# Attending the first batch in halves of queries, with early operands transposed by DMA and weights cast by GpSimd's DMA

## The chip, the cores and the metric

One core of one Trainium2 chip runs the kernel. The metric is the device time in microseconds (us) of one launch. All runs quoted are in the fast state, except where the text says otherwise. "Step" below is one exponential of 128 x 768 scores on ACT (ScalarE); a head pair of one batch takes 12 of them. PE is TensorE, DVE is VectorE, POOL is GpSimd, SP is SyncE (which only issues DMAs here).

## The reference, cut to what matters

Hash-bucketed attention feeds two matrix products ("the experts") with an activation between them.

```python
# q, k, v [4 batches, 8 heads, 768, 64], proj [64, 6]
q_bucket = sum_k 2**k * ((q @ proj)[..., k] > 0)        # likewise k_bucket
scores = where(q_bucket[:, None] == k_bucket[None, :], q @ k.T / 8, -1e9)
attn   = softmax(scores) @ v                            # -> x [3072, 512]
h      = x @ w_in                                       # w_in [512, 2048]
g      = h + sin(alpha * h)**2 / (alpha + 1e-9)
out    = g @ w_out                                      # w_out [2048, 512]
```

## The kernel before

There are 16 pairs (batch, two heads). For each, the kernel needs `qa` and `ka`: q and k transposed (64 rows), with 12 rows of hash bits and their complements appended, so that one matmul of 76 rows gives score and mask together. Pairs 0 to 5 are prepared on PE (hash, pick the bits, 24 transposes, four copies out of PSUM); later pairs are transposed by DMA while PE does other work. A batch's experts run after the first pair of the next batch has been attended, so before the first experts there are five pairs, 60 steps. The second product (`contract`) is dripped between the steps of the following batch by `fill`.

```python
def load_w(n):                       # 16 pieces, float32, issued by SP
    if n < 8:
        t = w_pool.tile([128, NP, 256], FP32, name="w32")
        ...
    nc.sync.dma_start(out=t, in_=src)
    return dst, t
def cast_w(dst, t, engine):          # engine is GpSimd
    engine.tensor_copy(out=dst, in_=t)

def prepare_on_pe(i):                # pairs 0 to 5
    ...                              # DVE turns q, k; GpSimd casts them into nat
    hash_into(ps, turned)            # 16 matmuls
    ...                              # DVE: bits; PE: 24 small matmuls pick rows; DVE: into nat
    for h in range(2):
        for t in (0, 1):
            out = ps[0:KA, t, 0:HALF].bitcast(BF16)
            for s in range(SB):
                nc.tensor.transpose(out[:, s * 128:(s + 1) * 128], nat[:, s, 2 * t + h], ident)
            nc.vector.tensor_copy(out=aug[t][0:KA, h, :], in_=out)
            yield
    ...

def attend(i, at_step, lag=3):
    for n in range(2 * SB):          # 12 steps
        hh, kb = divmod(n, SB)
        sc, _ = slot()               # two PSUM banks out of 0 to 5
        for half in range(2):
            nc.tensor.matmul(out=sc[:, half, 0:HALF],
                lhsT=ka[0:KA, hh, kb * 128:(kb + 1) * 128],
                rhs=qa[0:KA, hh, half * HALF:(half + 1) * HALF], start=True, stop=True)
        nc.scalar.activation(out=e..., in_=sc[:, :, 0:HALF], func=AF.Exp, scale=SCALE)
        at_step(n)                   # loads, preparation, second product
        ...                          # the exponential of three steps ago weighs v

def expand(b, at_chunk):             # first product and activation, 16 turns
    for F in range(NF):
        h = banks[:, 6:8, :] if F in (3, 7, 11) else slot()[0]
        ...                          # 8 matmuls, Sin, square, g

for i in range(n_pairs):
    attend(i, at_step)
    if hp == 0 and b > 0:
        drain()
        expand(b - 1, at_chunk)      # its last turn queues contract(b - 1)
```

The softmax here doesn't subtract the row's maximum and nothing guards it: scores larger than these inputs give would overflow.

## Time and profile before

| | us |
|---|---|
| median of 4 runs | 315.44 (312.86 to 318.0) |
| profiled span | 311.2 |
| first exponential | 10.7 |
| first matmul of the experts (after 60 steps) | 60.3 |
| next exponential | 85.5 |
| exponential number 108 (the first after batch 1's experts) | 156.7 |

The page of the kernel before, its parts 1, 2 and 4: busy time of each engine; then forty equal slices of the span with the busy share in tenths, the granted clock of PE and the share of the DMA engines; then the chain of waits by engine.

```profile
span 311.2 us, 7698 instructions
...
PE 300.7 (97%) x3055; PEld 184.3 (59%) x3055; DVE 203.5 (65%) x348; ACT 237.8 (76%) x295; POOL 97.4 (31%) x180
...
PE   7899999999989999999999999999999999999996
...
PEclk9999999999999999999999999999999999999999
DMA  7935989999628588881027587860013311200021
...
PE 73%; DVE 9%; DMA 5%; ACT 5%; POOL 3%; issue 2%; SPq 1%; DVEq 0%; ACTq 0%; POOLq 0%
```

PE is busy throughout (97%), 73% of the chain is PE.

The view by windows of the kernel before, cut at the stages of the table. Columns: window and its length, then busy us (and instructions) of each engine, granted clock, DMA share, GB/s.

```profile
core 0: us, PE busy (x) PEld busy (x) DVE busy (x) ACT busy (x) POOL busy (x), PEclk, DMA share, GB/s
0.00:10.70 10.70, 8.37 (x113) 7.25 (x114) 5.58 (x17) 2.29 (x4) 7.50 (x25) 1.00 0.85 278
10.70:60.30 49.60, 47.05 (x805) 34.20 (x804) 35.86 (x72) 43.95 (x59) 35.03 (x65) 1.00 0.83 222
60.30:85.50 25.20, 25.01 (x169) 14.66 (x166) 22.64 (x30) 22.94 (x27) 11.13 (x11) 1.00 0.89 265
85.50:156.70 71.20, 70.37 (x677) 41.51 (x676) 50.22 (x85) 59.45 (x73) 29.27 (x54) 1.00 0.57 133
156.70:311.20 154.50, 149.92 (x1303) 86.71 (x1300) 89.22 (x148) 109.16 (x135) 14.49 (x27) 1.00 0.34 83
```

### The profile page before, as it was taken

How to read it: one execution, taken by the hardware profiler on the slowest of the kernel's cores; microseconds unless marked ns; L12 is line 12 of the kernel's file. 1: busy time of each engine (PE TensorE's matmuls, PEld its weight loads, DVE VectorE, ACT ScalarE, POOL GpSimd, SP SyncE). 2: the span in 40 equal slices, each digit the busy share in tenths (PEclk: the TensorE clock that was granted, in tenths of full speed). 3: DMA queues.
4: the chain of work that ended last, by engine and by line, in shares of the span. 5: the costliest groups of instructions: out<-in, count | busy, mean ns of one | idle time of the engine just before them, and what ended most of it. 6: DMA issues, size and time to landing. Idle time of an engine off the chain costs nothing.

```text
span 311.2 us, 7698 instructions
## 1 busy us (share of the span) xinstructions
PE 300.7 (97%) x3055; PEld 184.3 (59%) x3055; DVE 203.5 (65%) x348; ACT 237.8 (76%) x295; POOL 97.4 (31%) x180
## 2 busy tenths in 40 slices
PE   7899999999989999999999999999999999999996
PEld 6567767666555565666555565566555655565444
DVE  5587576799956656679955744669974424499411
ACT  1679989899887787789897787789897877599200
POOL 6748398426594433515000524410000000000000
PEclk9999999999999999999999999999999999999999
DMA  7935989999628588881027587860013311200021
GB/s 238 377 126 138 241 276 282 185 290 293 209 71 223 94 220 207 148 225 26 2 69 194 122 223 127 205 115 7 2 56 51 105 28 69 59 2 0 35 102 68
DMA packets 68724, 42.87 MB, mean 138 GB/s; under 512 B 46560, under 2 KB 63696, under 8 KB 68688
## 3 DMA queue, kind: packets, MB, share of 16 engines
q1 hardware_dynamic: 68576, 42.37, 52.5%
q8 instruction: 24, 0.39, 0.6%
q14 instruction: 12, 0.10, 0.1%
q10 hardware_dynamic: 112, 0.01, 0.0%
HBM read 28.01 MB, written 7.27 MB: 113 GB/s over the span
## 4 chain that ended last, share of the span: by engine, by line
PE 73%; DVE 9%; DMA 5%; ACT 5%; POOL 3%; issue 2%; SPq 1%; DVEq 0%; ACTq 0%; POOLq 0%
PE banks L432 24%; PE banks L467 22%; PE banks L397 13%; PE banks L377 8%; ACT e L404 5%; PE banks L193 3%; DMA v_3085<-in_v_dram 2%; DVE g L419 2%; PE banks L269 2%; DVE osb L475 1%; DMA k_148<-in_k_dram 1%; DMA ka<-kn 1%; DMA xt<-xn 1%; DVE qt L184 1%; DVE xn L351 1%
## 5 line engine op out<-in xcount | busy, mean ns | idle before, releaser
L404 ACT ACTIVATE e<-banks 128x768 bf16<-128x768 f32 x192 | 147.6, 811 | 32.0 <-PE banks L397 24.2
L467 PE MATMUL banks<-w_out_bf,g 128*128 128x512 bf16 (+1 forms) x400 | 103.8, 370 | 1.4 <-DVE osb L475 1.0
L397 PE MATMUL banks<-qa,ka 76*128 76x384 bf16 x384 | 92.6, 325 | 1.4 <-DVE g L419 0.7
L432 PE MATMUL banks<-xt,w_in_bf 128*128 128x384 bf16 x512 | 85.3, 326 | 0.4 <-DMA xt<-xn 0.2
L377 PEld LDWEIGHTS <-e 128*128 128x128 bf16 x1152 | 55.2, 97 | 27.4 <-issue 0.3
L432 PEld LDWEIGHTS <-w_in_bf 128*128 128x128 bf16 x512 | 49.7, 98 | 33.8 <-issue 1.2
L441 ACT ACTIVATE s<-banks,alpha_sb 128x768 bf16<-128x768 f32 x64 | 57.1, 893 | 11.5 <-PE banks L432 10.6
L377 PE MATMUL banks<-vaug,e 128*128 128x65 bf16 x1152 | 61.5, 193 | 0.0
L467 PEld LDWEIGHTS <-g 128*128 128x128 bf16 x400 | 38.5, 97 | 33.5 <-issue 3.1
L345 DVE TENSOR_TENSOR total<-banks,base 128x390 f32<-128x390 f32 x28 | 15.7, 561 | 39.8 <-PE banks L377 39.6
L475 DVE COPY osb<-banks 128x512 f32<-128x512 f32 (+1 forms) x25 | 16.7, 668 | 28.4 <-PE banks L467 28.4
L397 PEld LDWEIGHTS <-ka 76*128 76x128 bf16 x384 | 28.5, 98 | 10.7 <-issue 2.0
L210 POOL TENSOR_TENSOR vacc<-vacc,vaug 128x130 f32<-128x130 f32 x48 | 21.5, 448 | 3.8
L351 DVE TENSOR_TENSOR xn<-total,rden 128x384 bf16<-128x384 f32 x28 | 17.3, 618 | 1.0
L193 PE MATMUL banks<-qt,w_hash 128*32 128x192 f32 x128 | 13.6, 332 | 1.3 <-ACT e L404 0.5
L193 PE MATMUL banks<-kt,w_hash 128*32 128x192 f32 x128 | 13.5, 332 | 0.0
L269 PEld LDWEIGHTS <-nat 128*76 128x76 bf16 x144 | 10.4, 114 | 3.7 <-POOL nat L228 0.8
L269 PE MATMUL banks<-ident,nat 128*76 128x128 bf16 x144 | 11.5, 219 | 1.1 <-DVE nat L256 0.7
L273 DVE COPY qa<-banks 76x768 bf16<-76x768 bf16 x12 | 6.5, 546 | 5.7 <-PE banks L269 5.7
L193 PEld LDWEIGHTS banks<-qt,w_hash 128*32 128x32 f32 x128 | 5.9, 109 | 7.4 <-issue 2.5
L309 DVE TENSOR_SCALAR bits<-banks,side 128x192 bf16<-128x192 f32 x20 | 7.4, 412 | 3.2 <-ACT e L404 3.2
L203 POOL CAST vaug<-v_2876 128x768 bf16<-128x768 f32 x1 | 0.8, 829 | 25.4 <-PE banks L377 25.4
(275 smaller groups left out, 289.4 us busy)
## 6 DMA issues: line engine op xcount, KB each, us to landing
out_dram<-osb SPq DMA_DIRECT2D x23, 256.0 KB
rows<-bits SPq DMA_DIRECT2D x40, 24.0 KB
w_697<-in_moe_w_in_dram SPq DMA_DIRECT2D x1, 512.0 KB
w_738<-in_moe_w_in_dram SPq DMA_DIRECT2D x1, 512.0 KB
w_921<-in_moe_w_in_dram SPq DMA_DIRECT2D x1, 512.0 KB
w_964<-in_moe_w_in_dram SPq DMA_DIRECT2D x1, 512.0 KB
w_1145<-in_moe_w_in_dram SPq DMA_DIRECT2D x1, 512.0 KB
w_1186<-in_moe_w_in_dram SPq DMA_DIRECT2D x1, 512.0 KB
```

The lines of the kernel that those rows point to most:

```text
L193: nc.tensor.matmul(out=ps[32 * j:32 * j + 32, 0:SB * 32].rearrange("p (s c) -> p s c", s=SB), lhsT=w_hash[:, blk].rearrange("p l a -> p (l ...
L210: nc.gpsimd.tensor_tensor(out=dst, in0=vacc[:, sb % 2], in1=vaug[:, :, sb], op=ALU.add)
L269: nc.tensor.transpose(out[:, s * 128:(s + 1) * 128], nat[:, s, 2 * t + h], ident)
L345: nc.vector.tensor_tensor(out=total, in0=cols, in1=operands[i][4][:, hh].unsqueeze(1).to_broadcast([128, SB, D + 1]), op=ALU.add,)
L351: nc.vector.tensor_tensor(out=xn[:, :, hh, :], in0=cols[:, :, 0:D], in1=rden.unsqueeze(2).to_broadcast([128, SB, D]), op=ALU.mult,)
L377: nc.tensor.matmul(out=regions[:, qb * (D + 1):(qb + 1) * (D + 1)], lhsT=e[:, qb * 128:(qb + 1) * 128], rhs=vaug[:, hh, kb, :], start=(apa ...
L397: nc.tensor.matmul(out=sc[:, half, 0:HALF], lhsT=ka[0:KA, hh, kb * 128:(kb + 1) * 128], rhs=qa[0:KA, hh, half * HALF:(half + 1) * HALF], s ...
L404: nc.scalar.activation(out=e.rearrange("p (h c) -> p h c", h=2), in_=sc[:, :, 0:HALF], func=AF.Exp, scale=SCALE,)
L432: nc.tensor.matmul(out=h[:, half, 0:HALF], lhsT=w_in_bf[:, p, F * 128:(F + 1) * 128], rhs=xt[b][:, p, half * HALF:(half + 1) * HALF], star ...
L441: nc.scalar.activation(out=s.rearrange("p (h c) -> p h c", h=2), in_=h[:, :, 0:HALF], func=AF.Sin, scale=alpha_sb[:, F:F + 1],)
L467: nc.tensor.matmul(out=o, lhsT=g[:, F, sub * 128:(sub + 1) * 128], rhs=w_out_bf[:, F, c0:c1], start=(F == 0), stop=(F == NF - 1),)
L475: nc.vector.tensor_copy(out=osb[:, c0:c1], in_=o)
```

## The change

The intent is to give PE the experts' work earlier and to take preparation off it. Its parts:

- Pairs 1 to 3 of batch 0 are attended in two passes, first for the first 384 queries, then for the others. The experts of the first half of the queries start after 39 steps instead of 60, those of the second half after another 21.
- All pairs after pair 0 are transposed by DMA; for pairs 1 to 3 the bit rows are put in place by small DMAs, straight from the chip's own memory.
- The weights are cast by GpSimd's DMA on their way in: 8 DMAs instead of 16 loads by SP with 16 casts.
- Pair 0 is loaded and prepared one head at a time; proj comes by four DMAs; 26 warm-up matmuls instead of 44.

The core of the diff, with cuts:

```diff
+    def cast_and_turn(i):                       # shortened: GpSimd casts, then
         for a, nat in zip(aug, nats):
             nc.sync.dma_start_transpose(out=a[:, 0, :]..., in_=nat...)
+    def prepare_early(i):                       # pairs 1 to 3, in six stages
+        ...                                     # DVE turns q and k, hash, bits
+        for a in range(4):
+            nc.tensor.matmul(out=ps[...], lhsT=spread[:, a]..., rhs=bits...)
+        move_second_head(i)
+        ...                                     # DVE copies the rows out of PSUM
+        for t in range(2):
+            for h in range(2):
+                nc.sync.dma_start(out=operands[i][t][D:KA, h, :], in_=rows[r0:r0 + 2 * NB]...)
...
     def load_w(n):
+        if n < 4:
+            nc.gpsimd.dma_start(out=w_in_bf[:, :, 512 * n:512 * (n + 1)], in_=moe_w_in[...])
...
-    def expand(b, at_chunk):
+    def expand(b, half=None):
...
+            pieces = ([(F, 0), (F, 1)] if half is None else [(F, half), (F + 1, half)])
+            turn = F if half is None else F // 2
+            h = banks[:, 6:8, :] if turn in (3, 7, 11) else slot()[0]
...
+    segments = [(0, None)] + [(i, h) for h in range(2) for i in range(1, NPAIR)]
+    segments += [(i, None) for i in range(NPAIR, n_pairs)]
...
+    stages(prepare_early, 2, [7, 8, 10, 11, 12, 14])
+    stages(prepare_early, 3, [13, 14, 16, 17, 18, 20])
+    place(12, lambda: load_w(2))
+    place(13, lambda: load_w(3))
+    for n, step in zip(range(4, 8), (20, 22, 24, 26)):
+        place(step, lambda n=n: load_w(n))
+    for i in range(NPAIR, n_pairs):
+        place({4: 18, 5: 26}.get(i, g0 - 42), lambda i=i: load(i))
...
+                if (i, half, n) == (2, 1, SB // 2 - 1):
+                    expand(0, 0)
+                    todo.append(contract(0, 0))
```

The first experts stand after 39 steps: 12 of pair 0, 6 for each of the three first halves, then 6 and 3 steps of second halves, under which the last outputs of the first half can be transposed.

## The prediction

> **What bounds the kernel now.** The page gives a span of 311.2 us; the chain of waits is 73% PE. PE's busy share (97%) overstates its work, so I count matmuls per window at the densest rate the chain shows: experts' first product (L432) 128 in 20.8 us = 0.1625 us each; second product (L467) 0.216; scores 0.1625; weighing (L377) 18 in 0.55; hash 16 in 0.79; early transposes (L269) 24 in 1.50; bit picking (L252) 24 in 0.33. Sum: about 289 us. The other 22 us:
> - 0 to 10.7 us, start: about 9
> - 10.7 to 60.5 us, 60 exponentials at 0.83 us a step (group "e": 811 ns): ACT sets the pace, PE has 44 us of work, 5 idle
> - 60.5 to 288 us: PE saturated, about 4 idle
> - the last 23 us: about 3 of draining
>
> So a change is worth the PE work and PE idleness it removes.
>
> **What it removes.** PE transposes and pickings of pairs 1 to 5: 5 x (1.50 + 0.33) = 9.2 us. It adds spread products (estimated 0.32 a pair, three pairs, 1 us) and empty-key matmuls (0.5). PE work falls by about 7.7 us. Experts begin after 39 steps instead of 60, but the work removed came from this phase, so idle PE there stays about the same (39 x 0.82 = 32 us with 25 of PE work: 6.5 idle).
>
> Start: one head gates the first scores, which halves a transposition (0.98 us) and 24 PE transposes; but proj now comes by four DMAs issued one after another (0.55 us each on ACT), so hashing starts no earlier than 5.97 us. First exponential near 9.9 us instead of 10.7.
>
> **What it adds.**
> - Batch 1 carries half a contraction: 48 steps, 38.5 us of PE against 39 of ACT: balanced, 1.5 lost
> - Half experts: two 384-column g updates (0.56 each, estimate from 1.015 for 768) and half a square per turn make DVE 1.35 us a turn against PE 1.30, plus a pair of table loads (1.28 each): 1.5 lost
> - DMA: weights and pairs 0 to 6 (17 MB, transposes more) are wanted by 55 us, where the queue moved 240 to 290 GB/s. [...] 2 us of stall for w_out allowed
> - GpSimd loses 16 casts of 1.0 to 1.4 us (off the chain), gains eight issues.
>
> **Sum.** 311.2 - 7.7 - 0.8 + 1.5 + 1.5 = 305.7 profiled, the stall partly hidden; unprofiled runs lie 2 to 5 us above. I predict 307 us, 8 in 10 within 300 to 314. Chances: faster by over 2% 0.57, same 0.35, slower 0.08.
>
> **What would show it.** First experts' matmul at 41 to 43 us instead of 60.5; L269's group down to 24 transposes; exponentials at 0.82 us a step before; an expert half 11 to 13 us; batch 1's 48 steps near 40 us instead of 49; later batches unchanged (21 us of experts, 49 of attention). Wrong if PE waits on w_in or w_out, or DVE on transposes of pairs 1 to 3.
>
> **What would make it wrong.** DMA unable to feed the shortened first phase (stalls of 5 us cancel the gain); GpSimd, in order, delivering values of pairs 1 to 3 late; or later batches speeding up through the new fill rates.

The 2 us of stall that it allowed is an estimate. Of the two small estimates in the 7.7 us, the 0.32 us of a pair's spread products is four matmuls of 192 columns at half of the 0.1625 us measured for 384 columns; the 0.5 us of the empty-key matmuls is not broken down.

## The result, and the profile after

The change made the kernel slower: a median of 350.99 us over 4 runs (348.92 to 352.84) against 315.44 us over 4 runs of the kernel before. The ratio is 1.1171 (95% interval 1.1097 to 1.1245). Ratios here are the mean time of one kernel's fast runs over the mean of the other's fast runs of the same rounds, so they are not quite the ratios of the medians quoted. The prediction was 307 us, with 300 to 314 as its range; both size and sign were wrong. (Of the four runs of the kernel before, its slowest, 318.0 us, lies 1.6% above its fastest, which is small beside 12%.)

The same parts of the page, kernel after:

```profile
span 349.6 us, 7324 instructions
...
PE 311.4 (89%) x2810; PEld 184.4 (53%) x2841; DVE 200.8 (57%) x375; ACT 242.6 (69%) x314; POOL 84.7 (24%) x167
...
PE   5996769495999769997998999999999999899996
...
PEclk9997855688999969999999999999999999999999
DMA  7999997833128134588740367695002232200022
...
PE 65%; DVE 12%; DMA 10%; issue 4%; ACT 3%; POOL 2%; SPq 2%; DVEq 0%; ACTq 0%; POOLq 0%
```

PE has its gaps in the first 15 slices (131 us), hardly any later. Its clock falls in the same slices (0.77 on average from 11.8 to 62.8 us). The DMA engines are full (9, 90% or more) from the second slice to the sixth and at 0.7 to 0.8 in the two after that. In the chain, DMA has doubled its share from 5% to 10% and the issuing ("issue", "SPq") has gone from 3% to 6%.

The view by windows of the kernel after, cut at its own stages, columns as before:

```profile
0.00:11.80 11.80, 7.07 (x73) 5.26 (x74) 5.49 (x24) 3.10 (x5) 6.10 (x19) 1.00 0.84 242
11.80:62.80 51.00, 41.81 (x418) 25.01 (x417) 21.87 (x52) 29.17 (x38) 28.84 (x58) 0.77 1.12 210
62.80:68.30 5.50, 0.69 (x6) 0.30 (x4) 0.35 (x1) 2.51 (x3) 1.61 (x2) 0.71 1.03 250
68.30:86.50 18.20, 14.27 (x92) 8.59 (x93) 14.27 (x27) 11.79 (x20) 4.76 (x9) 0.88 0.35 98
86.50:109.20 22.70, 22.53 (x227) 12.78 (x229) 8.78 (x21) 15.88 (x20) 4.57 (x9) 0.95 0.29 66
109.20:129.10 19.90, 15.07 (x95) 8.32 (x93) 15.84 (x30) 13.56 (x23) 4.85 (x9) 0.85 0.37 91
129.10:193.30 64.20, 60.86 (x624) 37.15 (x629) 44.80 (x76) 57.60 (x74) 19.74 (x36) 0.99 0.56 131
193.30:349.60 156.30, 149.06 (x1287) 87.01 (x1304) 89.43 (x148) 108.99 (x134) 14.24 (x27) 1.00 0.34 82
```

The DMA share can pass 1 because it adds up every packet's time, and packets overlap: the packet records have up to 36 open at once in the kernel after and up to 29 in the kernel before, for 16 engines (59.1% and 53.3% for the two queues of the kernel after in the DMA view below). Set beside the prediction's own terms, the stages give the whole loss:

| stage, us | before | after | predicted | after less predicted |
|---|---|---|---|---|
| start to first exponential | 10.7 | 11.8 | 9.9 | +1.9 |
| attention before the experts | 49.6 (60 steps) | 51.0 (39 steps) | 32 | +19.0 |
| PE waits for the experts' input | about 0.5 | 5.5 | 0 | +5.5 |
| experts, first half (before: all) | 24.7 | 18.2 | 12 | +6.2 |
| the next 21 steps | – | 22.7 | 22 | +0.7 |
| experts, second half | – | 19.9 | 12 | +7.9 |
| the next 48 steps and batch 1's experts | 71.2 | 64.2 | 62 | +2.2 |
| rest | 154.5 | 156.3 | 154.5 | +1.8 |

The predicted column adds up to 304.4, the after column to 349.6; the difference, 45.2 us, is the last column. (The prediction's 12 us is the middle of its 11 to 13, and 62 is its 40 us for the 48 steps and 22 for the experts. It gives no figure for the 21 steps between; 22 us is filled in afterwards, and its "21 us of experts" is rounded up to 22, so these two rows test it least.) Nearly all the loss lies before 130 us.

The 39 steps should take 0.82 us each. They went as follows: steps 0 to 6 took 9.3 us, 6 to 12 8.8, 12 to 18 8.6, 18 to 24 9.4, and the last 15 steps 14.9 us. Against 4.9 us for six steps and 12.3 for fifteen, that is 4.4, 3.9, 3.7, 4.5 and 2.6 us lost.

The chain of waits of the kernel after between 24 and 71 us, its longest links and where they lead. Columns: start, length, what.

```profile
24.09 5.17 DMA ka<-rows
...
29.30 0.50 PE banks L462 x2
...
44.26 9.89 DMA v<-in_v_dram
...
54.20 0.83 POOL vaug L213
...
57.56 0.82 POOL qn L301
...
59.72 3.62 DMA ka<-kn
...
63.53 4.71 DMA xt<-xn
68.28 1.76 PE banks L495 x5
```

First the 12 bit rows of a pair: a DMA of 18 KB takes 5.17 us and PE's scores (L462) wait for it. Then the values of pair 4: the load takes 9.89 us, GpSimd takes the values and only then casts q and k of that pair, SP transposes them, and only after that does SP issue the transposition that makes `xt`, the input of the experts. For it PE stood 4.8 us of the stage from 62.8 to 68.3 us.

The DMA view of 10 to 60 us, one fence for each kernel (queue, packets, MB, share of 16 engines), first before, then after:

```profile
q1 hardware_dynamic: 12617, 11.07, 82.0%
```

```profile
q1 hardware_dynamic: 10338, 6.68, 59.1%
q0 software_dynamic: 4224, 4.19, 53.3%
```

Queue 0 is GpSimd's. Its 4224 packets held 53.3% of 16 x 50 us, 426 us. The 4096 of them that carry weights took 104 ns on average (median 98), and each writes 1 KB of bfloat16 from 2 KB of float32. In the packet records of the kernel before, the plain packets of `w_in`, of 1 KB, took 51 ns on average (median 46), and those of `w_out`, of 2 KB, 96 ns (median 84). Hence the weights cost the DMA engines about the same in both forms: 4096 x 104 ns / 16 = 26.6 us of all sixteen after, (4096 x 51 + 2048 x 96) / 16 = 25.3 us before. What changed is when. Before, only `w_in` was asked for before 60 us, six of its eight pieces, and `w_out` came under the experts, issued from 65.5 to 80.5 us; after, all of `w_in` and, at 33 to 36 us, `w_out` are asked for before the experts.

### The profile page after: what moved, and what is told of

Read it like the earlier page. It is cut to its first block, busy times and chain, and to the rows that moved or that the text cites. A ratio compares the mean times of both kernels' runs of the same rounds, so it can differ in the third digit from the quotient of the medians.

```text
span 349.6 us, 7324 instructions
## 1 busy us (share of the span) xinstructions
PE 311.4 (89%) x2810; PEld 184.4 (53%) x2841; DVE 200.8 (57%) x375; ACT 242.6 (69%) x314; POOL 84.7 (24%) x167
## 3 DMA queue, kind: packets, MB, share of 16 engines
q0 software_dynamic: 4224, 4.19, 7.6%
## 4 chain that ended last, share of the span: by engine, by line
PE 65%; DVE 12%; DMA 10%; issue 4%; ACT 3%; POOL 2%; SPq 2%; DVEq 0%; ACTq 0%; POOLq 0%
PE banks L536 22%; PE banks L495 15%; PE banks L462 14%; PE banks L433 8%; DVE g L517 6%; DMA v<-in_v_dram 4%; PE banks L203 4%; DVE s L515 2%; DMA ka<-kn 2%; DMA ka<-rows 1%; ACT e L469 1%; DMA xt<-xn 1%; DVE total L398 1%; POOL vacc L220 1%; ACT s L510 1%
## 5 line engine op out<-in xcount | busy, mean ns | idle before, releaser
L462 PE MATMUL banks<-qa,ka 76*128 76x384 bf16 x384 | 102.6, 352 | 10.5 <-DMA ka<-rows 8.0
L536 PE MATMUL banks<-w_out_bf,g 128*128 128x512 bf16 (+1 forms) x369 | 100.9, 378 | 11.6 <-DVE g L517 8.5
L495 PE MATMUL banks<-xt,w_in_bf 128*128 128x384 bf16 x512 | 86.5, 328 | 6.9 <-DMA xt<-xn 4.8
L433 PEld LDWEIGHTS <-e 128*128 128x128 bf16 x1152 | 58.7, 102 | 30.3 <-issue 6.5
L495 PEld LDWEIGHTS <-w_in_bf 128*128 128x128 bf16 x512 | 49.9, 98 | 40.6 <-issue 8.8
L510 ACT ACTIVATE s<-banks,alpha_sb 128x768 bf16<-128x768 f32 (+1 forms) x80 | 59.1, 767 | 16.6 <-PE banks L495 15.7
L517 DVE SCALAR_TENSOR_TENSOR g<-s,inv_alpha,banks 128x768 bf16<-128x768 bf16 (+1 forms) x80 | 66.0, 852 | 5.8 <-ACT s L513 2.3
L433 PE MATMUL banks<-vaug,e 128*128 128x65 bf16 x1152 | 63.8, 199 | 1.6 <-DVE total L398 1.1
L536 PEld LDWEIGHTS <-g 128*128 128x128 bf16 x400 | 39.3, 99 | 45.0 <-issue 14.6
L213 POOL CAST vaug<-v 128x768 bf16<-128x768 f32 x16 | 13.3, 834 | 142.9 <-DMA v<-in_v_dram 96.9
L462 PEld LDWEIGHTS <-ka 76*128 76x128 bf16 x384 | 30.0, 103 | 24.1 <-DMA ka<-rows 8.8
L544 DVE COPY osb<-banks 128x512 f32<-128x512 f32 (+1 forms) x25 | 16.7, 669 | 44.8 <-PE banks L536 36.7
L513 ACT ACTIVATE s<-s 128x768 bf16<-128x768 bf16 x28 | 23.6, 843 | 0.9
L515 DVE TENSOR_TENSOR s<-s 128x768 bf16<-128x768 bf16 x36 | 21.3, 592 | 1.5 <-ACT s L510 1.5
L220 POOL TENSOR_TENSOR vacc<-vacc,vaug 128x130 f32<-128x130 f32 x48 | 21.1, 440 | 3.8
L203 PE MATMUL banks<-qt,w_hash 128*32 128x192 f32 x128 | 18.2, 381 | 2.2 <-POOL w_hash L134 1.9
L203 PE MATMUL banks<-kt,w_hash 128*32 128x192 f32 x128 | 17.7, 381 | 0.0
L403 DVE RECIPROCAL rden<-banks 128x3 f32<-128x3 f32 (+1 forms) x14 | 2.5, 178 | 25.3 <-PE banks L433 25.3
L192 DVE STREAM_TRANSPOSE qt<-q 128x768 f32<-128x768 f32 x15 | 14.6, 972 | 0.2
```

The lines of the kernel that those rows point to most:

```text
L203: nc.tensor.matmul(out=ps[32 * j:32 * j + 32, 0:SB * 32].rearrange("p (s c) -> p s c", s=SB), lhsT=w_hash[:, blk].rearrange("p l a -> p (l ...
L220: nc.gpsimd.tensor_tensor(out=dst, in0=vacc[:, sb % 2], in1=vaug[:, :, sb], op=ALU.add)
L433: nc.tensor.matmul(out=regions[:, qb * (D + 1):(qb + 1) * (D + 1)], lhsT=e[:, at:at + 128], rhs=vaug[:, hh, kb, :], start=(apart and kb == ...
L462: nc.tensor.matmul(out=sc[:, at, 0:HALF], lhsT=ka[0:KA, hh, kb * 128:(kb + 1) * 128], rhs=qa[0:KA, hh, hf * HALF:(hf + 1) * HALF], start=T ...
L495: nc.tensor.matmul(out=h[:, at, 0:HALF], lhsT=w_in_bf[:, p, f * 128:(f + 1) * 128], rhs=xt[b][:, p, hf * HALF:(hf + 1) * HALF], start=(p = ...
L510: nc.scalar.activation(out=s[:, at], in_=h[:, at, 0:HALF], func=AF.Sin, scale=alpha_sb[:, f:f + 1])
```

## The experiments

Four theories stood at the start. **A:** too many bytes are wanted too early; the DMA engines are full and everything that comes by DMA lands late. **B:** preparing pairs 1 to 3 by DMA is a long chain of small transfers, too slow for the six steps that it is given, whatever the load. **C:** the lower PE clock is a cause and not only a consequence of the gaps. **D:** attending and computing in halves costs more than thought. The kernels of one round ran on the same chip. Kernels that give a wrong result are named. All edits are against the kernel after, unless said otherwise.

### warm: 48 warm-up matmuls in place of 26 (theory C)

```diff
-        for _ in range(26):
+        for _ in range(48):
```

> Only the number of warm-up matmuls goes from 26 to 48. Clock theory (PE starts cold because its warm-up ends at 4.0 us and hashing begins at 6.0; at half clock the first 20 us and the waits stretch): the 12 first transposes take 0.75 us instead of 1.49, the first six exponentials are through 3 to 5 us earlier, the whole 345 to 347 us. DMA theory (late landings set the first 65 us): the start is faster but the experts' first matmul still comes at 60 us or later and the whole stays within 2 us of 351.

Measured: 357.31 us, ratio 1.1364 (1.1235 to 1.1494). Hashing ran at full speed now (a pair of matmuls every 0.16 us instead of every 0.32), and the first exponential came at 11.0 us instead of 11.8. But the clock fell again, to 0.50, at 10.0 us, after a stretch (6.6 to 10.0 us) in which PE was busy for 1.84 of 3.40 us, and step 6 came at 20.5 us against 21.1. In these runs the longer warm-up gained nothing. They do not settle theory C: `whole_late` below has the same program as `warm` up to step 6, kept the full clock there (1.00 from 4.5 to 25.0 us) and reached step 6 at 16.3 us.

### quarter: a quarter of the weights (wrong result; theory A)

```diff
     def load_w(n):
+        if n not in (0, 4):
+            return
-                        lhsT=w_in_bf[:, p, f * 128:(f + 1) * 128],
+                        lhsT=w_in_bf[:, p, (f % 4) * 128:(f % 4 + 1) * 128],
-                rhs=w_out_bf[:, F, c0:c1],
+                rhs=w_out_bf[:, F % 4, c0:c1],
```

> Wrong result on purpose: only 2 of the 8 weight loads are made, and the products read these for all chunks. DMA theory: without 6 MB of weight traffic in the first 65 us loads and transposes land in time, experts begin near 45 us instead of 63 to 68, the whole is 318 to 330 us. Clock theory: the cold start stays, the whole is above 340 us. Structure theory (half-width experts and their fill are what costs): above 340 us.

Measured: 345.67 us, ratio 1.0995 (1.0896 to 1.1093). The last exponential before the experts came at 54.0 us instead of 63.2, but PE then waited for `xt` until 61.8 us, so only about 6.5 us of the earlier start was left. Bytes matter; by themselves they are not the whole.

### whole: no halves, everything else kept (theory D)

```diff
-    segments = [(0, None)] + [(i, h) for h in range(2) for i in range(1, NPAIR)]
-    segments += [(i, None) for i in range(NPAIR, n_pairs)]
+    segments = [(i, None) for i in range(n_pairs)]
-        early = len([h for _, h in segments if h is not None]) // 2 + 2
+        early = NPAIR + 1
-                rate = 2.2 if b == 0 or i == NPAIR else (1.1 if b == 1 or i == 2 * NPAIR else 1.9)
+                rate = 1.9
         ...                            # the half experts are left out too
```

> Undoes the halves alone: batch 0 is attended in whole pairs, experts begin after 60 steps as before the change; DMA transposes, GpSimd weight casts and first pair by heads stay. DMA theory (demand pulled into too short a time): 312 to 325 us, since the same bytes have 20 steps more. Clock theory: about 345 us. Structure theory: about 335 us.

Measured: 339.96 us, ratio 1.0813 (1.0707 to 1.0919). This is the clearest single result. The experts (24.8 us) and batch 1 (71.8) took what they take in the kernel before (25.2 and 71.2), and the whole loss lies ahead of them: the 60 steps ended at 85.3 us instead of 60.3. The halves make matters worse, but most of the loss needs no halves. The time fits none of the three expectations as it stands.

### petrans: pairs 1 to 3 transposed by PE again (theory B)

```diff
     def prepare_early(i):
         ...
+        nat = early_nat[i]                                  # cast by GpSimd
+        ...                                                 # 24 picking matmuls, into nat
+        for h in range(2):
+            for t in range(2):
+                out = ps[0:KA, t, 0:HALF].bitcast(BF16)
+                for s in range(SB):
+                    nc.tensor.transpose(out[:, s * 128:(s + 1) * 128], nat[:, s, 2 * h + t], ident)
+                nc.vector.tensor_copy(out=operands[i][t][0:KA, h, :], in_=out)
-        ...                                                 # spread matmuls and row DMAs
```

> Pairs 1 to 3 are prepared with PE transposes and bit picking again (as before the change) instead of DMA transposes and row DMAs; halves, weight DMAs and first pair by heads stay (score buffers 6 instead of 8 for room). DMA theory: the 5 us waits for the row and transpose DMAs go, the experts begin 8 to 15 us earlier, the whole is 333 to 343 us. If queueing of these small DMAs is not the cause: 350 us or more, since PE has 7 us more of work.

Measured: 350.83 us, ratio 1.1158 (1.1051 to 1.1266). Step 30 came at 45.1 us instead of 54.0, nine microseconds earlier, and the gain was gone before the experts. The chain of waits of this run between 30 and 70 us, its two longest DMA links on the way to the experts:

```profile
36.85 15.99 DMA v<-in_v_dram
...
63.90 4.87 DMA xt<-xn
```

The faster steps reached the load of pair 4 sooner, that load then took 16 us, and `xt` came no earlier than before.

### filler: extra matmuls to hold the clock (theory C)

```diff
+            for _ in range(6 if b == 0 and (half != 1 or i == 1) else 0):
+                nc.tensor.matmul(out=sc[:, 1, HALF:HALF + 128], lhsT=empty, rhs=empty, start=True, stop=True)
-        for _ in range(26):
+        for _ in range(48):
```

> After every pair of score matmuls of the first 36 steps 6 matmuls of 128 columns into unused PSUM columns keep PE busy, and 48 warm-up matmuls stand before; nothing else changes. Cold-clock theory (with half clock PE itself paces steps 0 to 6, 12 to 18 and 24 to 36): PE stays at full clock in most of the first 60 us, exponential 6 comes at 17 to 18 us instead of 21.1, the experts begin 8 to 13 us earlier, the whole is 338 to 343 us. In-order-queue theory (waits for row DMAs and for v of pair 4 set the time): the waits grow by what PE gains, the whole is 347 to 355 us.

Measured: 352.74 and 359.70 us. The profiled run, 359.70 us, was slow, so there is no ratio and its profile is not compared. Inconclusive; nothing below rests on it.

### order: the loads of pairs 4 and 5 ahead of the weights (theory A, the queue's order)

```diff
-        place({4: 18, 5: 26}.get(i, g0 - 42), lambda i=i: load(i))
+        place({4: 9, 5: 19}.get(i, g0 - 42), lambda i=i: load(i))
```

> Only the places of the loads of pairs 4 and 5 in the SP queue change: steps 9 and 19 instead of 18 and 26. In-order-queue theory (v of pair 4 is issued at 44 us behind DMAs that wait for computation; GpSimd, SP and the transpose of xn for the experts wait behind it in turn): v lands before 40 us, the PE wait of 4.8 us for xt goes, the whole is 340 to 346 us. If DMA bandwidth rather than issue order is short: the row DMAs land later by as much, no gain (349 to 353).

Measured: 346.26 us in the profiled run; the other, 352.91 us, was slow, so there is no ratio. In the profile, the last exponential before the experts came at 59.5 us (63.2 in the kernel after) and PE still waited 3.84 us for `xt`. With the loads out of the way, each of the three pairs waited for its bit rows: DMAs of 4.82, 5.77 and 5.31 us, and six steps took 8.7 to 9.3 us.

### rowsact: the row DMAs on ACT's queue (theory B, a full queue as the cause)

```diff
-                nc.sync.dma_start(
+                nc.scalar.dma_start(
                     out=operands[i][t][D:KA, h, :],      # and one stage later
```

> Only the row DMAs of pairs 1 to 3 move from the SP queue to the ACT queue (and one stage later in the program, so that ACT needn't wait for their source). In-order-queue theory: they overtake the loads and transposes queued on SP, land in about 2 us instead of 5, PE's two waits of 4 to 5 us for them shrink to under 1, the whole is 340 to 346 us. Bandwidth theory: they still take 4 to 5 us and the whole stays at 349 to 353.

Measured: 356.07 us, ratio 1.1339 (1.1306 to 1.1372). On ACT's queue the last row DMA, issued at 52.00 us, still took 6.88 us, and the exponentials on ACT stood 12.0 us in two gaps behind ACT's own row issues. So SP's queue alone did not make these transfers slow. Nor did the transfer start early on that other queue: the 12 packets of the last row DMA took 65 to 75 ns each, but all 12 started at 57.0 to 57.9 us, over 4 us after their issue had ended at 52.75. Where they waited is not shown.

### three: the edits of filler, order and rowsact together

> All three together. If the causes are the cold clock, issue order of loads and queueing of row DMAs, and they add: experts begin at 45 to 50 us, the whole is 322 to 332 us. If one hides another: 332 to 340. If none is the cause: above 345.

Measured: 357.71 us, ratio 1.1392 (1.1332 to 1.1451). It combined one edit that hurt (rowsact), filler and one that may help (order); a miss that tells nothing new.

### ahead: preparation begun earlier (theory B)

```diff
-    stages(prepare_early, 1, [0, 1, 3, 5, 6, 7])
+    stages(prepare_early, 1, [0, 0, 1, 2, 3, 4])
-    stages(prepare_early, 2, [7, 8, 10, 11, 12, 14])
-    stages(prepare_early, 3, [13, 14, 16, 17, 18, 20])
+    stages(prepare_early, 2, [5, 6, 6, 7, 8, 9])
+    stages(prepare_early, 3, [11, 12, 12, 13, 14, 15])
         ...                            # with order; pair 3 cast in the setup
```

> Preparation of pairs 1 to 3 is moved ahead by 1 to 5 steps in the program (spread products and row DMAs at steps 3, 8 and 14 instead of 6, 12 and 18), pair 3 is cast and transposed before the second weight load, and pairs 4 and 5 are loaded at steps 9 and 19. Latency-loop theory (each pair's row DMA is issued only after the first step of the pair before it, and spread, copy, four issues and landing take 9 us where six steps take 5): six steps of pairs 1 to 3 take 5 to 7 us instead of 9, experts begin at 48 to 55 us instead of 63 to 68, the whole is 330 to 340 us. If DMA throughput sets the landings whatever the order: 345 or more.

Measured: 347.46 us, ratio 1.1089 (1.0972 to 1.1206). Step 30 came at 50.1 us instead of 54.0, and the first exponential after the first half's experts at 82.9 instead of 86.5: a small gain, of the size that order's profile showed.

### norows: no row DMAs at all (wrong result; theory B)

```diff
-                nc.sync.dma_start(
-                    out=operands[i][t][D:KA, h, :],
-                    in_=rows[r0:r0 + 2 * NB].rearrange("p s a c -> p (s a c)"),
-                )
+                nc.vector.memset(operands[i][t][D:KA, h, :], 0.0)
```

> Wrong result on purpose: the row DMAs of pairs 1 to 3 are replaced by clearing the same rows on VectorE, so the hash bits never arrive; all else stays. Latency-loop theory: steps 12 to 30 take about 6 us per six instead of 8 to 9, the two PE waits for ka<-rows (9.9 us together) go, experts begin 8 to 12 us earlier, and the whole is 337 to 343 us. If these waits are hidden behind other late DMAs: within 3 us of 351.

Measured: 353.03 us, ratio 1.1267 (1.1115 to 1.1419). The waits for rows were gone and step 30 came at 43.8 us, ten microseconds earlier. The experts hardly gained: PE then waited for `xt` until 66.2 us (68.3 in the kernel after), and the next exponential came at 86.0 against 86.5. Its chain of waits between 30 and 66 us shows why, and it is petrans' story again:

```profile
37.02 15.29 DMA v<-in_v_dram
...
61.65 4.50 DMA xt<-xn
```

Theory B is right about the waits for rows, and wrong that they alone set the time: behind them stands another late DMA.

### bank: the half experts' eighth turn leaves banks 6 and 7 alone (theory D)

A half has 8 turns. Turn 7, its last, takes banks 6 and 7, and the second product that follows writes bank 7. In the whole version turn 7 is followed by eight more.

```diff
-            h = banks[:, 6:8, :] if turn in (3, 7, 11) else slot()[0]
+            h = banks[:, 6:8, :] if turn in ((3, 7, 11) if half is None else (3,)) else slot()[0]
```

> In half experts only turn 3 uses PSUM banks 6 and 7 for its first product, no longer turn 7, the last one, whose banks the second product needs at once. Bank theory (PE stands 3.9 us after each half expert until VectorE has read the last turn out of bank 7, and the clock drops): each half is 3 to 5 us shorter, the whole is 342 to 346 us. If VectorE's own pace is what makes halves long (structure theory): no change, 349 to 353.

Measured: 343.94 us, ratio 1.0977 (1.0855 to 1.1098), so some 6 us better than the change (the two intervals only just do not overlap). The timeline of PE around the end of the first half's experts, first in the kernel after, then in this run. Columns: start, length of the group, instructions, and in brackets the idle time before it and what ended it.

```profile
75.83 5.04 PE L495 MATMUL banks<-xt,w_in_bf 128*128 128x384 bf16 x30
84.74 1.11 PE L536 MATMUL banks<-w_out_bf,g 128*128 128x512 bf16 x3 [3.87 <-DVE g L517]
```

```profile
82.78 1.46 PE L495 MATMUL banks<-xt,w_in_bf 128*128 128x384 bf16 x8 [0.17 <-DVE g L517]
84.07 1.03 PE L536 MATMUL banks<-w_out_bf,g 128*128 128x512 bf16 x4
```

After, PE stands 3.87 us until DVE has read turn 7's result out of bank 7 and the second product (L536) may begin, and the clock halves (0.50 from 85.5 to 89.0 us). Here the second product follows at once. On the measure of the table of stages, the first half took 15.3 us (71.0 to 86.3) instead of 18.2 and the second 13.9 (107.6 to 121.5) instead of 19.9. In both kernels the first 3 us of the first half go to five matmuls of the experts at half the usual pace (1.76 us, 0.35 each where the densest rate before is 0.1625; in the kernel after the clock reads 0.50 from 65.1 to 71.9 us) and to matmuls left over from the attention; without these 3 us it took 12.3 us here and 15.2 in the kernel after.

### petrans_quarter: the edits of petrans and of quarter together (wrong result; A and B)

> Wrong result on purpose: PE preparation of pairs 1 to 3 together with a quarter of the weight loads; apart, the first gave 350.8 and the second 345.7. If the row and transpose DMAs and the weight traffic are two limits side by side, each hiding what the other gives: together 330 to 338 us. If they simply add, 345.

Measured: 342.05 us, ratio 1.0917 (1.0802 to 1.1031). The last exponential before the experts came at 50.5 us instead of 63.2; neither part had given that alone (54.0 and 60.9). PE then waited for `xt` until 57.7 us.

### whole_pe, whole_pe_hw, fix, fix_quarter: several repairs at once

Single repairs hid each other, so this round undoes several things in one kernel. `whole_pe` is whole and petrans with the loads of pairs 4 and 5 at steps 6 and 18. `whole_pe_hw` also loads the weights by SP in 16 pieces with casts on GpSimd, as the kernel before does, but with two staging buffers instead of three. `fix` keeps the halves: petrans, bank, 48 warm-ups, loads of pairs 4 and 5 at steps 9 and 24, and casts ahead of the values. `fix_quarter` is `fix` with a quarter of the weights (wrong result).

```diff
-        place({4: 18, 5: 26}.get(i, g0 - 42), lambda i=i: load(i))    # whole_pe: on top of
+        place({4: 6, 5: 18}.get(i, g0 - 42), lambda i=i: load(i))     # whole and petrans
...
+    w_pool = ctx.enter_context(tc.tile_pool(name="w32", bufs=2))      # whole_pe_hw: on top of
+        nc.sync.dma_start(out=t, in_=src)                             # whole_pe
+            dst, t = held_w.popleft()
+            nc.gpsimd.tensor_copy(out=dst, in_=t)
...
     def prepare(i):                     # fix; whole_late and whole_pe_late too
-        values[i] = take_values(i)
-        yield
         turned = [turn_blocks(name, loaded[i, name]) for name in ("q", "k")]
         cast_and_turn(i)
         ...
+        values[i] = take_values(i)
+        yield
...
-        place({4: 18, 5: 26}.get(i, g0 - 42), lambda i=i: load(i))
+        place({4: 9, 5: 24}.get(i, g0 - 34), lambda i=i: load(i))
```

> Halves and early DMA preparation both undone (pairs 1 to 3 prepared by PE, whole pairs, experts after 60 steps, pairs 4 and 5 loaded at steps 6 and 18 as before the change); first pair by heads and weights by GpSimd DMA stay. Theory that the loss comes from halves and early DMA preparation together, which only hide each other: 312 to 320 us, near before. If the weights by GpSimd DMA or the first pair by heads (with the cold PE clock at the start) carry a large part: 325 to 340.

Measured: 333.09 us, ratio 1.0633 (1.0556 to 1.071). Step 30 came at 43.9 us (54.0 in the kernel after, 36.9 before), then pair 4 waited: the issue of its transposition on SP, at 45.48 us, lasted 7.92 us.

> As whole_pe, and the weights come again in 512 KB pieces by the SP queue, two per pair and the rest during the experts, cast by GpSimd. If the weights' GpSimd DMA, issued 4 MB at a time beside the loads, is a cause of its own: 8 us or more faster than whole_pe. If not: within 4 us of it. Both near 314 would leave the first pair by heads harmless.

Measured: 348.22 us, ratio 1.1116 (1.1088 to 1.1144). GpSimd waited 43.5 us for weight pieces and SP waited for GpSimd's casts. The two buffers are the likely new bottleneck, so the run is a miss: it doesn't tell whether weights by GpSimd's DMA are worse than by SP.

> Halves kept; pairs 1 to 3 by PE, PSUM banks of turn 7 as in bank, pairs 4 and 5 loaded at steps 9 and 24, later pairs eight steps later than in the change, cast and transpose of a pair ahead of its values on GpSimd, 48 warm-up matmuls. If row DMAs, load order, banks and FIFO behind loads are the causes: experts begin at 45 to 52 us, the whole is 318 to 328 us. If DMA throughput under the weights is the limit left: experts begin after 55 us, the whole is 330 to 340.

Measured: 338.44 us, ratio 1.0809 (1.075 to 1.0868). Steps 0 to 6 took 6.2 us (9.3 in the kernel after), with the clock full; the last exponential before the experts came at 46.6 us. PE then waited for `xt` until 55.5 us.

> Wrong result on purpose: fix with a quarter of the weight loads. If DMA throughput is what is left in fix: 10 us or more faster than fix and experts begin at 43 to 47 us. If not: within 3 us of fix.

Measured: 325.17 us, ratio 1.0388 (1.0265 to 1.051), 13.3 us less than `fix`. The two ran alike to 46.6 us; there `fix_quarter` went on at once. SP's timeline of `fix`, then of `fix_quarter`, at the same three issues (start, length, instruction):

```profile
39.79 8.74 SPq L303 DMA_TRANSPOSE qa<-qn  x1
48.63 2.50 SPq L303 DMA_TRANSPOSE ka<-kn  x1
51.22 1.95 SPq L417 DMA_TRANSPOSE xt<-xn  x1
```

```profile
39.67 1.23 SPq L305 DMA_TRANSPOSE qa<-qn  x1
41.00 1.46 SPq L305 DMA_TRANSPOSE ka<-kn  x1
42.56 1.21 SPq L419 DMA_TRANSPOSE xt<-xn  x1
```

The same transposition of pair 4 takes SP 8.74 us to issue in one and 1.23 us in the other. SP issues in order, so `xt`, which PE waits for, is issued at 51.22 us instead of 42.56. The DMA view of 10 to 60 us, of the same two kernels:

```profile
q0 software_dynamic: 4224, 4.19, 53.7%
q1 hardware_dynamic: 9201, 6.70, 50.0%
```

```profile
q1 hardware_dynamic: 11556, 7.64, 54.7%
q0 software_dynamic: 1056, 1.05, 13.4%
```

The shares add up to more than 100% in the first and to 68% in the second. A packet of queue 0 takes about 101 ns in both (13.4% of 800 us over 1056 packets), so it isn't the crowding that makes it long. This pair of runs shows theory A in this much: with all else equal, three quarters of the weights cost 13 us (the interval of the ratio makes that about 4 us more or less; the two profiled runs differ by 11.1 us). The edit takes away bytes, packets and GpSimd's issues together, so the pair does not tell which of these delays SP. What `fix_quarter` has left over the kernel before is partly of its own making: like `fix`, it has the loads of pairs 6 to 15 eight steps later, and GpSimd waited 32.6 us for q from 96 to 168 us, and batch 1 took 71.2 us instead of 64.2 (70.8 in `fix`).

### whole_late and whole_pe_late: the weights spread out in time

Both are without halves, with 48 warm-ups, casts ahead of the values and the loads of pairs 4 and 5 at steps 6 and 18. `whole_late` prepares pairs 1 to 3 by DMA, `whole_pe_late` by PE.

```diff
-    place(12, lambda: load_w(2))
-    place(13, lambda: load_w(3))
+    place(24, lambda: load_w(2))
+    place(34, lambda: load_w(3))
-    for n, step in zip(range(4, 8), (20, 22, 24, 26)):
+    for n, step in zip(range(4, 8), (48, 51, 54, 57)):
```

> Halves undone; DMA preparation of early pairs, first pair by heads and GpSimd weight DMAs kept, but the weights spread: w_in at the start and at steps 24 and 34, w_out at steps 48 to 57 instead of 20 to 26; pairs 4 and 5 loaded at steps 6 and 18, casts of a pair ahead of its values, 48 warm-up matmuls. Timing theory (the change's 8 MB of weights within the first 60 us, beside loads and transposes, is what delays them; whole gave 340): experts begin at 62 to 70 us instead of 85, the whole is 312 to 324 us. If early DMA preparation itself is too slow at any load: above 330.

Measured: 335.39 us, ratio 1.0673 (1.0619 to 1.0727); one of the four runs, 337.91 us, was slow and is not in the ratio. This is above 330, where the expectation puts early preparation by DMA as too slow at any load: PE waited for row DMAs of 6.19 and 7.42 us for pairs 1 and 2, and step 12 came at 28.9 us against 22.4 in the kernel before.

> The same weights, loads, casts and warm-up with pairs 1 to 3 prepared by PE (whole_pe gave 333). Timing theory: pair 4's transposes, whose issue stood 7.9 us in whole_pe under w_out, go out at once, experts begin at 60 to 64 us, the whole is 310 to 318 us. If GpSimd weight DMAs hurt at any time: above 325.

Measured: 331.19 us, ratio 1.0562 (1.0502 to 1.0623). This is the fastest correct version, still 5.6% above the kernel before. It is also above the 325 us at which the expectation blamed GpSimd's weight DMAs at any time; that rival was not tested further. The experts and batch 1 are as before (25.2 us and 71.2 us); 15.3 us of the 17.5 us lost lie ahead of them, and its chain of waits between 40 and 64 us says where:

```profile
51.37 6.56 DMA rows<-bits
...
59.16 3.01 DMA ka<-rows
```

Step 42 came at 49.5 us (46.7 before) and step 48, the first of pair 4, at 63.1 (51.2 before), so 9.1 us of the 15.3 were lost between these two. In this version pair 4 still goes through DMA for its transposition and for its bit rows, which the kernel before did on PE. The bit rows alone went to memory in 6.56 us and came back in 3.01 us, and SP had taken 6.87 us for the four issues of the first of these. The clock was halved behind the gap: 0.50 from 63.1 to 75.6 us, with PE busy all the time.

### Marks of the runs

Starts of exponentials, us; "ready" is the last one before the experts, "next" the first after the (half) experts, "108" the first after batch 1's experts.

| run | ratio | 6 | 30 | ready | next | 108 |
|---|---|---|---|---|---|---|
| before | 1 | 16.7 | 36.9 | 60.3 | 85.5 | 156.7 |
| after | 1.1171 | 21.1 | 54.0 | 63.2 | 86.5 | 193.3 |
| quarter* | 1.0995 | 20.2 | 47.8 | 54.0 | 80.0 | 187.8 |
| petrans | 1.1158 | 21.1 | 45.1 | 60.9 | 87.8 | 193.1 |
| petrans_quarter* | 1.0917 | 20.4 | 44.3 | 50.5 | 75.9 | 184.4 |
| norows* | 1.1267 | 20.3 | 43.8 | 60.4 | 86.0 | 192.6 |
| bank | 1.0977 | 21.1 | 54.9 | 63.8 | 86.3 | 186.1 |
| fix | 1.0809 | 16.5 | 40.4 | 46.6 | 71.1 | 177.0 |
| fix_quarter* | 1.0388 | 16.5 | 40.4 | 46.6 | 60.8 | 167.4 |
| whole | 1.0813 | 21.3 | 47.1 | 85.3 | 110.1 | 181.9 |
| whole_pe | 1.0633 | 19.9 | 43.9 | 78.9 | 103.6 | 175.1 |
| whole_late | 1.0673 | 16.3 | 45.3 | 79.7 | 104.4 | 175.6 |
| whole_pe_late | 1.0562 | 16.6 | 40.6 | 75.6 | 100.8 | 172.0 |

(* wrong result.)

## Why the prediction was wrong

**"PE work falls by about 7.7 us ... idle PE there stays about the same": this step failed.** The view of what limits the kernel was right for the kernel before: PE, with hardly a gap. The prediction took that for a property of the stage. But the change took work from PE and gave it to the DMA engines, in the one stage where they were already at 0.83. The stage's new limit was what to compute.

**"DMA: ... 17 MB ... wanted by 55 us, where the queue moved 240 to 290 GB/s ... 2 us of stall for w_out allowed": this is the term that was mis-sized most.** Its own numbers contradict it: 17 MB at 240 to 290 GB/s takes 59 to 71 us. An estimate in engine time says the same: the kernel before used 0.85 x 10.7 + 0.83 x 49.6 = 50 us of all 16 engines by 60 us. The last quarter of `w_in` adds 3 us, which makes about 54 us for a stage meant to end at 42; `w_out` adds 12 us, which makes 66 us by 55 us, when the prediction wants it. Measured in the kernel after: 0.84 x 11.8 + 1.12 x 51.0 = 67 us by 62.8 us, PE stands 4.8 us for `xt`, and `fix` is 13.3 us faster with a quarter of the weights. GpSimd's queue and SP's took 53.3% and 59.1% of the time of 16 engines in the same 50 us; the prediction named the contention but drew no number from it.

**"32 us" for 39 steps, "exponentials at 0.82 us a step": wrong, 51.0 us.** Of the 19 us, 4.4 went in the first six steps, 12.1 between steps 6 and 24, and 2.6 in the rest.

- In steps 6 to 24 the largest cause is the row DMAs of pairs 1 to 3, which the prediction didn't cost at all. For pair 1, DVE's copies (1 us), two of the four issues (1.8 us) and 5.2 us to landing make 8 us, against the 5 us that six steps should last; the stage ran at 8.6 to 9.4 us per six steps. Without the row DMAs (norows) these 18 steps took 19.2 us instead of 26.8. So the rows explain 7.6 of the 12.1 us. About 4.4 us are left, and petrans, where PE prepares these pairs, keeps them too (19.8 us); what they are was not taken apart. Fewer weights did not make pair 1's row DMA faster: with a quarter of them it still took 4.99 us (quarter). That the experts gained only 2 us in norows shows the two causes standing one behind the other.
- In the first six steps it is the clock for the most part. The pairs of hash matmuls start every 0.32 us, in the run warm every 0.16 us. The first clock record of the trace is at 20.7 us, so the page's 1.00 until then is not evidence. But two other traces show it: warm and whole_late run the same program up to step 6. In warm the clock was 0.50 from 10.0 to 23.7 us and steps 0 to 6 took 9.5 us; in whole_late it was 1.00 from 4.5 to 25.0 us and they took 6.0 us. In the kernel after they took 9.3. No edit decided which of the two happened. Why the clock fell in one and not in the other is not shown. So part of a start-up's speed was luck, and step 6 at 16.3 to 16.6 us (fix, fix_quarter, whole_late, whole_pe_late) is not the merit of 48 warm-ups alone.
- In the last 15 steps PE was busy all the time (14.9 of 14.9 us from 47.9 to 62.8) at a clock of 0.54, so their 2.6 us go with the clock as well; why it stayed low is not shown.

**"First exponential near 9.9 us": 11.8.** Hashing began at 6.0 us, as predicted, but at half speed (a pair of matmuls every 0.32 us): the shorter warm-up had ended at 4.0 us, and with the longer one (warm) a pair took 0.16 us.

**"An expert half 11 to 13 us": 18.2 and 19.9 us.** Without the bank conflict (bank) the halves took 15.3 and 13.9 us, the first of them 12.3 us without its first 3 us, so the costs of smaller pieces were nearly right. What failed is that the prediction didn't follow the rule `turn in (3, 7, 11)` into a loop of 8 turns, where turn 7 is the last and its bank is the one that the second product needs. With both of these stalls the clock fell: PE stood 3.87 us until 84.7 us and 4.60 us until 124.9 us, and the clock read 0.50 from 85.5 to 89.0 and from 123.1 to 129.9 us. In all, the clock read 0.50 for 6.8, 17.1, 6.8, 3.4 and 6.8 us between 30 and 130 us.

**What was right.** PE bounds the kernel before. Batch 1's 48 steps took 40.1 us (predicted near 40; 47.1 before), so the intended gain is real: batch 1 with its experts fell from 71.2 to 64.2 us. The later batches did not change (156.3 against 154.5 us), and the PE transpositions fell to pair 0's 24. "Wrong if PE waits on w_in or w_out, or DVE on transposes of pairs 1 to 3" looked in the right place; but PE waited for row DMAs (8.0 us) and for `xt` (4.8 us), which stood behind other issues on SP, not for the weights.

**What stays open.** The effects do not add, so no split of the 36.6 us lost by step 108 is claimed: repairs of single causes (quarter, petrans, norows, ahead, bank) gained at most 6 us each; in the traces of quarter, petrans and norows the next late DMA took over. Why the best version is still 15.3 us late is argued from its trace (9.1 us at pair 4, by DMA under load, and 3.4 us after it at half the clock), and no run put pairs 4 and 5 back on PE. Whether the weights would be better loaded by SP and cast by GpSimd stays open too, since `whole_pe_hw` starved itself. That SP's issue lasts 8.74 us because its queue was full is an inference; shown is only that it shrinks to 1.23 us with fewer weights. None of the versions tried beat the kernel before.

## What to carry to other kernels

Before a stage is shortened, add up the DMA engines' time that must be over before the stage's end, from the share column of the kernel before, and compare it with the shortened stage: here about 54 us were asked of 42, and 66 of 55. Here work was moved from a busy PE to DMA engines that were already at 0.83, and that lost time. A small DMA on the way to a matmul took 4.8 to 7.4 us for pairs 1 to 3, so it needs a lead counted in time and not in steps. If single repairs gain nothing, several causes may stand one behind the other: undo them together, then take one away.

## What the traces show of the hardware

- A casting packet of GpSimd's DMA, of 1 KB written, took 104 ns on average, about as much as a plain one of 2 KB (96 ns) and twice a plain one of 1 KB (51 ns): here the time went with the bytes read.
- The issue of a DMA transposition once took 8.74 us on SP (fix; 7.92 us in whole_pe), 1.23 us with a quarter of the weights (fix_quarter), and delayed all that SP issued after it. How long an issue can last is not shown.
- Small DMAs in the crowded phase: row transfers of 18 KB for pairs 1 to 3 on which PE waited took 4.8 to 7.4 us to land on SP's queue and 6.9 us on ACT's. Later ones, read from device memory, took 1.6 to 1.7 us (whole at 139.7 us, warm at 161.6 us).
- The clock fell after a stretch of 3.4 us with PE busy for 1.84 us and no gap above about 0.65 us (warm, 6.6 to 10.0 us). No threshold of busy time comes out of the traces: it held after stretches with 1.92 us (whole_pe_late, 5.1 to 8.5 us) and 2.17 (before, 5.5 to 8.9 us), and fell after one with 2.23 (ahead, 24.5 to 27.9 us).
- Before a profile's first clock record the clock row gives 1.00. In the kernel after that record is at 20.7 us, yet pairs of hash matmuls started every 0.32 us at 6 us, and every 0.16 us in the run with the longer warm-up.
